# Linformer decode on one core: two heads per tile on 64 partitions each, K in 512-column matmuls, V multiplied by p·F

## Chip, cores, metric

One core of one Trainium2 chip. The metric is the device time of one execution in microseconds (us). The "span" of a profile runs from the first to the last instruction of one execution; the time is about 2 us longer than the span. "PE" is TensorE; its "granted clock" is the share of its full clock that it was given.

## The reference

```python
B, H, Sq, Skv, Dh, R = 2, 16, 1, 8192, 256, 8          # all bf16
kp = einsum("rn,bhnd->bhrd", e_proj, k)                # E K : 8 x 256 per head
vp = einsum("rn,bhnd->bhrd", f_proj, v)                # F V : 8 x 256 per head
scores = einsum("bhqd,bhrd->bhqr", q, kp) * Dh ** -0.5 # 8 scores per head
o = einsum("bhqr,bhrd->bhqd", softmax(scores), vp)
```

There are 32 heads. Each has 4.19 MB of K and 4.19 MB of V, 268.4 MB in all, read once. Everything else is small. Note that p·(F V) = (p·F) V: once the 8 probabilities of a head are known, F can be folded to one weight per row of V.

## The kernel before

Sixteen pairs of heads. Four buffers of 32 KB per partition hold one head's K or V each, as 128 partitions x 64 rows x 256. Per pair they hold K0, K1, V1, V0 (c = 0..3), and a buffer is loaded again when its matmuls are done.

```python
for a in range(NPAIR):                      # SyncE: the loads
    for c in range(NS):                     # NS = 4
        if a >= 1: nc.sync.wait_ge(s_rd[c], a)
        if ...: nc.sync.dma_start(out=big[:, c], in_=src).then_inc(s_dma[c], 16)      # 4 MB
        else:   # last pair: pieces, g1="32,32", g2="32,16,16", g3="16,12,10,8,6,4,3,2,1,1,1"
            ...
with nc.tensor.Fori(0, NPAIR) as it:        # TensorE
    ...                                     # q matmul
    for c in range(NS):
        ...                                 # waits
        for gi, gs in enumerate(groups[c]):
            for _ in range(gs):
                if c < 2:      # K: E.T k, 256 columns
                    mm = matmul(acc_k[:, c*Dh:(c+1)*Dh], lhsT=wT[:, j, 0:R2:2], rhs=big[:, c, j, :], ...)
                elif c == 2:   # V of head 1: F.T v  -- needs no probabilities
                    mm = matmul(acc_v1, lhsT=wT[:, j, 1:R2:2], rhs=big[:, c, j, :], ...)
                else:          # V of head 0: (p.F) v -- needs the softmax
                    mm = matmul(o_ps[0], lhsT=wp[:, j:j+1], rhs=big[:, c, j, :], ...)
            if c == 2 and gi == 0: ...      # broadcast p of head 0 to 128 partitions (pb)
            if c == 3 and gi == 0: ...      # o of head 1 = p (F v)
        mm.then_inc(s_rd[c], 1)
```

VectorE (DVE) makes the scores, ScalarE the exponential, and DVE then multiplies F by p and sums over the 8 ranks (wtmp, wp32, wp). This chain runs while TensorE (PE) works on c = 2.

Of the kernel before, what the change touches and what calls it, by code (L numbers as in the profile page):

```python
# [13 lines left out]
CFG = dict(g1="32,32", g2="32,16,16", g3="16,12,10,8,6,4,3,2,1,1,1")  # L14
# [3 lines left out]
def kernel(  # L18
# [8 lines left out]
):  # L27
    nc = tc.nc
# [4 lines left out]
    assert Sq == 1 and Skv % P == 0  # L33
    J = Skv // P
    BH = B * H
    G = 2
    assert BH % G == 0 and G * Dh <= 512
    NPAIR = BH // G
    assert 2 <= NPAIR <= P
    R2 = 2 * R  # L40
    NS = 4
    scale = float(Dh) ** -0.5
    TQ = 32

    CH = (P // 2) // R
    assert R * CH * 2 == P and Skv % CH == 0
    XW = Skv // CH
    PIECE = min(XW, 512)
    assert XW % PIECE == 0
    NPIECE = XW // PIECE  # L50
# [3 lines left out]

    big = sb.tile([P, NS, J, Dh], BF16, name="kv")
    wT = sb.tile([P, J, R2], BF16, name="wT")
    st = sb.tile([P, XW], BF16, name="ef_stage")
    sel_ef = sb.tile([P, CH, R2], BF16, name="sel_ef")
    q16 = sb.tile([NPAIR, G * Dh], BF16, name="q16")
    sel_q = sb.tile([NPAIR, NPAIR, R], BF16, name="sel_q")  # L60
    q_sb = sb.tile([R, G * Dh], BF16, name="q_sb")
    ident_b = sb.tile([R2, R2], BF16, name="ident_b")
    sc_in = sb.tile([TQ, TQ], FP32, name="sc_in")
    sc_out = sb.tile([TQ, TQ], FP32, name="sc_out")
    p_in = sb.tile([TQ, TQ], FP32, name="p_in")
    p_out = sb.tile([TQ, TQ], FP32, name="p_out")
    prod = sb.tile([R, G, Dh], FP32, name="prod")
    nmax = sb.tile([G, 1], FP32, name="nmax")
    ssum = sb.tile([G, 1], FP32, name="ssum")
    rsum = sb.tile([G, 1], FP32, name="rsum")  # L70
    p_pv = sb.tile([R, G], BF16, name="p_pv")
    vp_sb = sb.tile([R, Dh], BF16, name="vp_sb")
    ones1 = sb.tile([1, P], FP32, name="ones1")
    wtmp = sb.tile([P, J, R], FP32, name="wtmp")
    wp32 = sb.tile([P, J], FP32, name="wp32")
    wp = sb.tile([P, J], BF16, name="wp")
    o_all = sb.tile([1, BH * Dh], BF16, name="o_all")

    wps = pp.tile([P, J, R2], BF16, name="wps")
    NB = 6  # L80
    banks = [pp.tile([R2, 512], FP32, name=f"bank{i}") for i in range(NB)]
    pb_t = pp.tile([P, R], FP32, name="pb")
    acc_k = banks[0][0:R, 0:G * Dh]
    acc_v1 = banks[1][0:R, 0:Dh]
    o_ps = [banks[2][0:1, 0:Dh], banks[3][0:1, 0:Dh]]
    q_ps = banks[4][0:R, 0:G * Dh]
    pb = pb_t[:]

    ef_sb = big[:, NS - 1].rearrange("p j d -> p (j d)")[0:R2, 0:Skv]

    k_h = k.rearrange("b h (p j) d -> (b h) p j d", p=P)
    v_h = v.rearrange("b h (p j) d -> (b h) p j d", p=P)
    q_pr = q.rearrange("b h s d -> (b h s) d").rearrange("(a g) d -> a (g d)", g=G)
    o_v = out.rearrange("b h s d -> s (b h d)")
    e_st = e_proj.rearrange("r (c x) -> (r c) x", c=CH)
    f_st = f_proj.rearrange("r (c x) -> (r c) x", c=CH)

    def parse(key, fallback):
        tp = [int(x) for x in CFG[key].split(",")]
        return tp if sum(tp) == J else fallback  # L100

    def geometric():
        tp, rem = [], J
        while rem > 0:
            s_ = max(1, (rem * 3) // 10)
            tp.append(s_)
            rem -= s_
        return tp

    half = [J // 2, J - J // 2] if J >= 2 else [J]  # L110
    groups = [[J], parse("g1", half), parse("g2", half), parse("g3", geometric())]
    assert all(sum(g_) == J for g_ in groups)

    with tc.tile_critical(name="main"):
        sem = lambda n: nc.alloc_semaphore(f"lr_{n}")
        s_dma = [sem(f"dma{s}") for s in range(NS)]
        s_grp = [[sem(f"g{c}_{i}") for i in range(len(groups[c]))] for c in range(NS)]
        s_rd = [sem(f"rd{s}") for s in range(NS)]
        s_st, s_q, s_mm, s_qb, s_k0 = sem("st"), sem("q"), sem("mm"), sem("qb"), sem("k0")
        s_out = [sem(f"out{i}") for i in range(2)]  # L120
        s_pool, s_dve, s_act, s_tr = sem("pool"), sem("dve"), sem("act"), sem("tr")
        s_pv, s_pb = sem("pv"), sem("pb")

        cnt = {"dve": 0, "act": 0, "mm": 0}
        ND, NA = 11, 5

        def dve(inst):
            inst.then_inc(s_dve, 1)
            cnt["dve"] += 1
            return cnt["dve"]  # L130

        def act(inst):
            inst.then_inc(s_act, 1)
            cnt["act"] += 1
            return cnt["act"]

        npool = 0
        nc.gpsimd.memset(sel_ef[:], 0.0).then_inc(s_pool, 1); npool += 1
        nc.gpsimd.memset(sel_q[:], 0.0).then_inc(s_pool, 1); npool += 1
        nc.gpsimd.memset(ident_b[:], 0.0).then_inc(s_pool, 1); npool += 1  # L140
        nc.gpsimd.wait_ge(s_pool, npool)
        nc.gpsimd.affine_select(
            out=sel_ef[:], in_=sel_ef[:], compare_op=ALU.not_equal, fill=1.0,
            base=0, pattern=[[-1, CH], [-CH, R], [-(P // 2), 2]], channel_multiplier=1,
        ).then_inc(s_pool, 1); npool += 1
        NPOOL_EF = npool
        nc.gpsimd.affine_select(
            out=ident_b[:], in_=ident_b[:], compare_op=ALU.not_equal, fill=1.0,
            base=0, pattern=[[-1, R2]], channel_multiplier=1,
        ).then_inc(s_pool, 1); npool += 1  # L150
        NPOOL_ID = npool
        nc.gpsimd.affine_select(
            out=sel_q[:], in_=sel_q[:], compare_op=ALU.not_equal, fill=1.0,
            base=0, pattern=[[1, NPAIR], [0, R]], channel_multiplier=-1,
        ).then_inc(s_pool, 1); npool += 1
        nc.gpsimd.memset(sc_in[:], 0.0).then_inc(s_pool, 1); npool += 1
        nc.gpsimd.memset(p_in[:], 0.0).then_inc(s_pool, 1); npool += 1
        nc.gpsimd.memset(ones1[:], 1.0).then_inc(s_pool, 1); npool += 1
        NPOOL = npool

        while cnt["dve"] < ND:
            nc.vector.sem_inc(s_dve, 1)
            cnt["dve"] += 1

        bank_busy = [None] * 4
        nc.tensor.wait_ge(s_st, 32)
        nc.tensor.wait_ge(s_pool, NPOOL_EF)
        for c in range(CH):
            for h in range(NPIECE):
                i = cnt["mm"]  # L170
                b = i % 4
                if bank_busy[b] is not None:
                    eng, c_ = bank_busy[b]
                    nc.tensor.wait_ge(s_act if eng == "act" else s_dve, c_)
                nc.tensor.matmul(banks[b][0:R2, 0:PIECE], lhsT=sel_ef[:, c, :], rhs=st[:, h * PIECE:(h + 1) * PIECE],  # L175
                                 start=True, stop=True).then_inc(s_mm, 1)
                cnt["mm"] += 1
                dst = ef_sb[:, c * XW + h * PIECE:c * XW + (h + 1) * PIECE]
                if i % 2 == 0:
                    nc.scalar.wait_ge(s_mm, cnt["mm"])  # L180
                    bank_busy[b] = ("act", act(nc.scalar.copy(out=dst, in_=banks[b][0:R2, 0:PIECE])))
                else:
                    nc.vector.wait_ge(s_mm, cnt["mm"])
                    bank_busy[b] = ("dve", dve(nc.vector.tensor_copy(out=dst, in_=banks[b][0:R2, 0:PIECE])))  # L184

        nc.tensor.wait_ge(s_pool, NPOOL_ID)
        nc.tensor.wait_ge(s_act, cnt["act"])
        nc.tensor.wait_ge(s_dve, cnt["dve"])
        tr = None
        for j in range(J):  # L190
            tr = nc.tensor.transpose(out=wps[:, j, :], in_=ef_sb[:, j::J], identity=ident_b[:])  # L191
        tr.then_inc(s_tr, 1)
        nc.scalar.wait_ge(s_tr, 1)
        act(nc.scalar.copy(out=wT[:], in_=wps[:]))  # L194
        A0 = cnt["act"]
        D0 = cnt["dve"]
        assert A0 + 1 - NA >= 0 and D0 + 1 - ND >= 0

        def tile_src(a, c):
            return (k_h[a * G + c] if c < 2 else v_h[a * G + (3 - c)])  # L200

        def out_dma(a_lo, a_hi, i):
            nc.sync.wait_ge(s_act, A0 + (a_hi - 1) * NA + 5)
            nc.sync.dma_start(out=o_v[:, a_lo * G * Dh:a_hi * G * Dh],
                              in_=o_all[:, a_lo * G * Dh:a_hi * G * Dh]).then_inc(s_out[i], 16)

        J0 = min(J // 8, J - 1) if NPAIR > 1 else 0
        if J0 > 0:
            nc.sync.dma_start(out=big[:, 0, 0:J0, :], in_=k_h[0][:, 0:J0, :]).then_inc(s_k0, 16)
        nc.sync.dma_start(out=st[0:P // 2, :], in_=e_st).then_inc(s_st, 16)  # L210
        nc.sync.dma_start(out=st[P // 2:P, :], in_=f_st).then_inc(s_st, 16)
        A_OUT = NPAIR - 2
        n_out = 0
# [168 lines left out]
```

## Time and profile before

| | before |
|---|---|
| time | 634.64 us, median of 3 (634.34 to 635.01) |
| span of the profile | 632.7 us |
| DMA in the middle | 431 to 432 GB/s |
| PE busy / mean granted clock | 82% / 0.943 |
| 4 MB transfer, issue to landing | 31 us |

From the page of the kernel before: the span, the busy time of PE, the forty slices (granted clock, DMA busy share, GB/s), the three costliest groups (busy us, mean ns of one, then the idle time before them and what ended it) and the issues of the large transfers.

```profile
span 632.7 us, 9355 instructions
...
PE 516.4 (82%) x4240; PEld 372.5 (59%) x4240; DVE 69.2 (11%) x184; ACT 39.6 (6%) x106; POOL 2.1 (0%) x13
...
PEclk9798999889989999989989999899899889988999
DMA  8999999999999999999999999999999999999996
GB/s 345 430 430 431 431 431 431 429 431 431 431 431 436 433 431 433 433 433 435 433 433 435 433 431 433 431 431 431 431 431 431 431 431 431 431 431 431 424 423 263
...
L266 PE MATMUL bank_85<-kv,wT 128*8 128x256 bf16 x2048 | 244.9, 284 | 46.9 <-DMA kv<-in_k_dram 46.9
...
L269 PE MATMUL bank_86<-kv,wT 128*8 128x256 bf16 x1024 | 124.8, 283 | 32.8 <-DMA kv<-in_v_dram 32.8
L272 PE MATMUL bank_87<-kv,wp 128*1 128x256 bf16 x1024 | 123.3, 280 | 25.2 <-DMA kv<-in_v_dram 23.5
...
kv<-in_k_dram SPq DMA_DIRECT2D x30, 4096.0 KB, 31.4
```

DMA is busy everywhere (share 1.00 and 432 and 431 GB/s in the two stretches of the middle shown below). All three matmul groups wait for transfers; the only other wait that the waits view gives them is 1.8 us for ScalarE (L272). One 4 MB transfer per 9.7 us is the pace: 38.9 us a pair.

Instructions in order of time (start us, duration us, engine, line, operation, shapes, count, idle before and its releaser), last pair of the kernel before:

```profile
599.77 14.13 PE L266 MATMUL bank_85<-kv,wT 128*8 128x256 bf16 x128 [1.77 <-DMA kv<-in_k_dram]
613.94 0.68 DVE L300 SCALAR_TENSOR_TENSOR prod<-bank_85,q_sb 8x512 f32<-8x512 f32 x1 [26.18 <-PE bank_85 L266]
...
614.44 3.65 PE L269 MATMUL bank_86<-kv,wT 128*8 128x256 bf16 x32 [0.54 <-DMA kv<-in_v_dram]
...
621.89 1.91 PE L272 MATMUL bank_87<-kv,wp 128*1 128x256 bf16 x16
...
623.92 5.90 PE L272 MATMUL bank_87<-kv,wp 128*1 128x256 bf16 x48
...
629.86 0.36 ACT L351 CAST o_all<-bank_87 1x256 bf16<-1x256 f32 x1 [5.46 <-PE bank_87 L272]
```

The chain starts at 613.94, and PE is on V from 614.44. PE starts on the last buffer at 621.89 and follows its small pieces; it is done at 629.8, and only the output's copy and store follow. The landing of the first V piece at 614.44, plus 6 MB at the stream's pace (14.6 us), puts the last landing at about 629.0. This is an estimate; by the trace the stream moves 58 GB/s from 628 to 629 us and 2 GB/s from 629 to 630.

### The profile page before, as it was taken

What the parts mean: (1) busy time and instruction counts of PE and PEld (TensorE: products, weight loads), DVE (VectorE), ACT (ScalarE), POOL (GpSimd) and SP (SyncE); (2) the same over time, 40 slices, a digit from 0 to 9 for tenths busy, and PEclk for the clock granted to TensorE, in tenths of its full rate; (3) what the DMA queues carried; (4) which work ended last, traced back from release to release, by engine and by line L of the source; (5) the groups of instructions that cost most, each with busy time, mean ns of one, the idle gap of its engine ahead of it and who ended that gap; (6) DMA issues with size and microseconds to landing.
All of it is one profiled execution on the core that took longest, in us unless ns stands there. A gap on an engine that the chain in (4) does not pass through costs nothing.

```text
span 632.7 us, 9355 instructions
## 1 busy us (share of the span) xinstructions
PE 516.4 (82%) x4240; PEld 372.5 (59%) x4240; DVE 69.2 (11%) x184; ACT 39.6 (6%) x106; POOL 2.1 (0%) x13
## 2 busy tenths in 40 slices
PE   5998788787787887897886878969868788687898
PEld 2666556566565664665655656646656556465675
DVE  3020100202002020110201002010020100201011
ACT  3100010000100001000000000000000000000100
POOL 1000000000000000000000000000000000000000
PEclk9798999889989999989989999899899889988999
DMA  8999999999999999999999999999999999999996
GB/s 345 430 430 431 431 431 431 429 431 431 431 431 436 433 431 433 433 433 435 433 433 435 433 431 433 431 431 431 431 431 431 431 431 431 431 431 431 424 423 263
DMA packets 11434, 268.80 MB, mean 425 GB/s; under 512 B 1298, under 2 KB 1954, under 8 KB 2851
## 3 DMA queue, kind: packets, MB, share of 16 engines
q1 hardware_dynamic: 11428, 268.74, 99.1%
q8 instruction: 2, 0.03, 0.0%
q14 instruction: 4, 0.03, 0.0%
HBM read 268.71 MB, written 0.02 MB: 425 GB/s over the span
## 4 chain that ended last, share of the span: by engine, by line
DMA 72%; PE 26%; issue 1%; DVE 0%; ACT 0%; SPq 0%
DMA kv<-in_v_dram 71%; PE bank_86 L269 20%; PE bank_85 L266 3%; PE bank_87 L272 1%; PE wps L191 1%; PE pb L277 1%; DMA ef_stage<-in_f_proj_dram 1%; DVE kv L184 0%; PE bank_85 L175 0%; PE bank_88 L175 0%; PE bank_87 L175 0%; PE bank_86 L175 0%; ACT wT L194 0%; PE bank_89 L250 0%; SPq L210 0%
## 5 line engine op out<-in xcount | busy, mean ns | idle before, releaser
L266 PE MATMUL bank_85<-kv,wT 128*8 128x256 bf16 x2048 | 244.9, 284 | 46.9 <-DMA kv<-in_k_dram 46.9
L266 PEld LDWEIGHTS bank_85<-kv,wT 128*8 128x8 bf16 x2048 | 182.6, 90 | 109.4 <-DMA kv<-in_k_dram 29.1
L269 PE MATMUL bank_86<-kv,wT 128*8 128x256 bf16 x1024 | 124.8, 283 | 32.8 <-DMA kv<-in_v_dram 32.8
L272 PE MATMUL bank_87<-kv,wp 128*1 128x256 bf16 x1024 | 123.3, 280 | 25.2 <-DMA kv<-in_v_dram 23.5
L269 PEld LDWEIGHTS bank_86<-kv,wT 128*8 128x8 bf16 x1024 | 90.0, 90 | 63.1 <-ACT p_in L317 30.2
L272 PEld LDWEIGHTS bank_87<-kv,wp 128*1 128x1 bf16 x1024 | 85.4, 86 | 60.0 <-issue 25.5
L300 DVE SCALAR_TENSOR_TENSOR prod<-bank_85,q_sb 8x512 f32<-8x512 f32 x16 | 10.9, 678 | 476.6 <-PE bank_85 L266 476.6
L317 ACT ACTIVATE p_in<-sc_out,nmax 2x8 f32<-2x8 f32 x16 | 4.8, 299 | 309.4 <-DVE nmax L310 309.4
L333 DVE TENSOR_TENSOR wtmp<-wT,pb 128x512 f32<-128x512 bf16 x16 | 11.0, 687 | 54.5 <-PE pb L277 54.5
L345 ACT CAST vp_sb<-bank_86 8x256 bf16<-8x256 f32 x16 | 5.8, 362 | 125.7 <-PE bank_86 L269 125.7
L336 DVE TENSOR_REDUCE wp_81<-wtmp 128x64 f32<-128x512 f32 x16 | 11.0, 686 | 0.5
L351 ACT CAST o_all<-bank_87 1x256 bf16<-1x256 f32 x16 | 5.8, 362 | 82.1 <-PE bank_87 L272 82.1
L304 DVE TENSOR_REDUCE sc_in<-prod 8x2 f32<-8x512 f32 x16 | 10.8, 674 | 0.6
L348 ACT CAST o_all<-bank_88 1x256 bf16<-1x256 f32 x16 | 5.8, 362 | 57.2 <-PE bank_88 L281 57.2
L294 ACT CAST q_sb<-bank_89 8x512 bf16<-8x512 f32 x16 | 9.2, 575 | 2.6 <-PE bank_89 L250 1.0
L175 PE MATMUL bank_85<-ef_stage,sel_ef 128*16 128x512 bf16 x4 | 2.3, 584 | 6.2 <-DMA ef_stage<-in_f_proj_dram 6.2
L250 PE MATMUL bank_89<-q_65,sel_q 16*8 16x512 bf16 x16 | 6.2, 387 | 1.4 <-ACT wT L194 1.4
L277 PEld LDWEIGHTS pb<-p_in,ones_79 1*128 1x128 f32 x32 | 4.7, 182 | 3.5 <-issue 3.3
L191 PE MATMUL wps<-ident_b,kv 16*128 16x16 bf16 x64 | 5.8, 230 | 0.9 <-DVE kv L184 0.9
L191 PEld LDWEIGHTS wps<-ident_b,kv 16*128 16x128 bf16 x64 | 5.8, 206 | 1.2 <-issue 1.2
L277 PE MATMUL pb<-p_in,ones_79 1*128 1x8 f32 x32 | 6.1, 262 | 0.0
L281 PE MATMUL bank_88<-vp_sb,p_pv 8*1 8x256 bf16 x16 | 4.7, 291 | 0.0
(36 smaller groups left out, 49.2 us busy)
## 6 DMA issues: line engine op xcount, KB each, us to landing
kv<-in_k_dram SPq DMA_DIRECT2D x30, 4096.0 KB, 31.4
kv<-in_v_dram SPq DMA_DIRECT2D x30, 4096.0 KB, 31.0
kv<-in_k_dram SPq DMA_DIRECT2D x2, 2048.0 KB, 29.1
kv<-in_k_dram SPq DMA_DIRECT2D x1, 3584.0 KB, 12.4
kv<-in_v_dram SPq DMA_DIRECT2D x3, 1024.0 KB, 26.7
kv<-in_v_dram SPq DMA_DIRECT2D x1, 2048.0 KB, 24.6
kv<-in_v_dram SPq DMA_DIRECT2D x1, 768.0 KB, 25.6
kv<-in_v_dram SPq DMA_DIRECT2D x1, 640.0 KB, 26.7
```

Of the source, the lines that this page charges most:

```text
L191: tr = nc.tensor.transpose(out=wps[:, j, :], in_=ef_sb[:, j::J], identity=ident_b[:])
L250: nc.tensor.matmul(q_ps, lhsT=sel_q[:, bass.ds(it, 1), :].rearrange("k a m -> k (a m)"), rhs=q16[:], start=True, stop=True).then_inc(s_qb, 1)
L266: mm = nc.tensor.matmul(acc_k[:, c * Dh:(c + 1) * Dh], lhsT=wT[:, j, 0:R2:2], rhs=big[:, c, j, :], start=(j == 0), stop=(j == J - 1))
L269: mm = nc.tensor.matmul(acc_v1, lhsT=wT[:, j, 1:R2:2], rhs=big[:, c, j, :], start=(j == 0), stop=(j == J - 1))
L272: mm = nc.tensor.matmul(o_ps[0], lhsT=wp[:, j:j + 1], rhs=big[:, c, j, :], start=(j == 0), stop=(j == J - 1))
L277: nc.tensor.matmul(pb, lhsT=ones1[0:1, :], rhs=p_in[0:1, 0:R], start=True, stop=True).then_inc(s_pb, 1)
L294: assert act(nc.scalar.copy(out=q_sb[:], in_=q_ps)) == A + 1
L300: assert dve(nc.vector.scalar_tensor_tensor(out=prod[:].rearrange("r g d -> r (g d)"), in0=acc_k, scalar=scale, in1=q_sb[:], op0=ALU.mult, ...
L304: dve(nc.vector.reduce_sum(out=sc_in[0:R, 0:G], in_=prod[:], axis=AX.X))
L333: assert dve(nc.vector.tensor_tensor(out=wtmp[:], in0=fT, in1=pb.unsqueeze(1).to_broadcast([P, J, R]), op=ALU.mult)) == D + 9
L336: assert dve(nc.vector.reduce_sum(out=wp32[:], in_=wtmp[:], axis=AX.X)) == D + 10
L345: assert act(nc.scalar.copy(out=vp_sb[:], in_=acc_v1)) == A + 3
```

## The change

Its intent: fewer and larger instructions, loops on ScalarE and VectorE as on TensorE, one accumulator for all outputs. A tile now holds two heads, each on 64 partitions with 128 rows per partition. K and V each have one buffer of 64 KB per partition, loaded as two halves of 32 KB that are released separately. K takes two rows per matmul (512 columns). V of both heads is multiplied by p·F. Core of the diff (set-up of E and F, the chain's details and semaphores cut):

```diff
-CFG = dict(g1="32,32", g2="32,16,16", g3="16,12,10,8,6,4,3,2,1,1,1")
+STEADY = (64, 64)
+LAST_V = (64, 24, 16, 10, 6, 4, 2, 2)
...
-    big = sb.tile([P, NS, J, Dh], BF16, name="kv")          # J = 64
+    kt = sb.tile([P, J, Dh], BF16, name="kt")               # J = 128
+    vt = sb.tile([P, J, Dh], BF16, name="vt")
...
+        nc.sync.dma_start(out=st[:, 0:R // 2, :], in_=e_v).then_inc(s_st, 16)   # 256 B pieces, were 2 KB
...
+        for a in range(NP):
+            for i, js in enumerate(STEADY):
+                if a > 0: nc.sync.wait_ge(s_kr[i], a)
+                load(kt, k_t[a], lo, j0 + js - lo, s_kd[i])
...         # the same for vt with s_vr; last pair: pieces LAST_V
+        with nc.tensor.Fori(0, NP) as it:
+            ...
+            for j in range(0, J, 2):
+                if j in steady_at: nc.tensor.wait_ge(s_kd[steady_at[j]], tk)
+                mm = nc.tensor.matmul(acc_k[:], lhsT=wk[:, j:j + 2, :]..., rhs=kt[:, j:j + 2, :]..., ...)
+                if j + 2 in steady_end: mm.then_inc(s_kr[steady_end[j + 2]], 1)
+            nc.tensor.wait_ge(s_p, t1)
+            ...                                             # pb: broadcast p, then
+            nc.tensor.wait_ge(s_w, t1)                      # the whole chain
+            for j in range(J):
+                ...
+                mm = nc.tensor.matmul(o_ps[:], lhsT=wp[:, j, :], rhs=vt[:, j, :], start=False, ...)
+                if j + 1 in steady_end: mm.then_inc(s_vr[steady_end[j + 1]], 1)
...
+        with nc.scalar.Fori(0, NP) as it:                   # were written out
+        with nc.vector.Fori(0, NP) as it:
```

## The prediction

> **What bounds it now.** The DMA engines. By the forty slices, DMA is 9 tenths or more busy nearly everywhere and moves 431-433 GB/s[...]. 268.4 MB of K and V at 431.5 GB/s are 622 us of the 632.7 us span. The pace is one 4 MB transfer per 9.72 us, 38.9 us per pair of heads. PE (82% busy by the page) waits for K or V in every tile by the waits view (46.9, 32.8 and 23.5 us), so it isn't the bound. Transfers are issued some 31 us before they land (DMA issues), so the queue is three deep.
>
> **What the change does not touch.** Bytes, 4 MB transfers, 32 KB per partition, four buffers. [...]I expect the same 9.7 us per transfer.
>
> **What it changes.**
> 1. K: 64 matmuls of 512 columns for 128 of 256. The old pitch is 14.13 us/128 = 110 ns; I estimate 217 ns for 512 columns: 13.9 us a pair, as before.
> 2. V: both heads now need softmax(p) times F before their first matmul. Before, the tile of F matmuls (3.65 us per 32) ran during the softmax chain, hiding it. Now PE stands still from the last K matmul to the first V matmul. Chain, from DVE durations of before: 0.68 + 0.67 + 0.20 + three small ones 0.5, exp 0.30, three small ones 0.55, broadcast matmuls 0.6, product and sum over F twice as wide (0.69 each for 512 elements; estimate 1.22 each for 1024), two copies 0.5, gaps: about 7.3 us.
> 3. [...]In this trace 32 matmuls after 2.8 us idle took 5.32 us against 3.65: add about 1.9 us per pair.
> 4. PE per pair: 13.9 + 14.1 + 0.5 + 7.3 + 1.9 = 37.7 us against 38.9 of DMA. So the middle stays DMA bound, just barely, and should cost nothing.
> 5. Start: projections come as 256 B pieces, not 2 KB (1024 packets of them)[...]. The quicker set-up of weights (PE begins K at 14-15 us, not 21) gains nothing, since DMA bounds.
>
> **The tail is on the critical path.** Before, the last V piece is used 0.4 us after landing; landing pace puts that at about 629 us. In the new order the last K half lands two transfers earlier, near 609.6 (+1.5). Then K matmuls 7.0, chain 7.3, 128 V matmuls 16.0 end at 639.9 (+1.5), some 10 us after the last byte; output copy and store 2.9 as before. Span 642.8 + 1.5 = 644.3 against 632.7; the time is 1.9 above the span.
>
> **Prediction: 646.5 us (+1.9%), 8 in 10 between 641 and 654.** Chances: faster 0.03, within 2% 0.55, slower 0.42 (the limit is 647.3).
>
> **Right if:** windows in the middle show 431 GB/s and a 38.9 us period; in the last 35 us DMA goes quiet about 10 us before the last V matmul; the chain of waits ends in PE V matmuls preceded by DVE products and sums, not by a V transfer; the granted clock dips at each V start. **Wrong if:** the middle's GB/s falls (PE and chain period over 38.9: each excess us costs up to 16), or the 64 KB row stride in HBM slows reading; then over 650. If the chain is shorter, or PE stays at full clock, 641-644.
>
> What could mislead me: chain steps twice as wide are scaled, not measured; the 256 B pieces have no counterpart in this trace; the clock after idle varies between tiles (5.32 or 3.65 us).

The sum came to 609.6 + 7.0 + 7.3 + 16.0 = 639.9 us for the end of V, 642.8 us with copy and store, 644.3 us with the 1.5 us more at the start, and 646.2 us with the 1.9 us between span and time. The reason for the 1.5 us, the 256 B pieces, was a guess, tested in experiment 5. For the other 1.9 us, those of the slow start, the trace of before shows 5.32 - 3.65 = 1.67 us in the example given, and 15.98 - 14.13 = 1.85 us for the first 128 K matmuls, from 21.25 us (granted clock 0.50 from 20.7 to 24.1 us). That the rate of the stream could not rise was not shown; slices of experiment 6 moved 442 GB/s.

## The result

After: 645.95 us, median of 4 (644.67 to 646.32), beside 634.49 us (4 runs) for the kernel before on the same chip. The ratio is 1.0176, interval 1.0162 to 1.0191: slower, clear of the noise, though under 2%. The prediction, 646.5 (+1.9%), was right.

From the page of the kernel after, the parts shown before:

```profile
span 642.9 us, 7074 instructions
...
PE 498.4 (78%) x3185; PEld 317.6 (49%) x3185; DVE 97.3 (15%) x225; ACT 16.2 (3%) x36; POOL 8.5 (1%) x13
...
PEclk9979989797997979989798897979979798897989
DMA  8999999999999999999999999999999999999990
GB/s 337 434 427 434 432 430 432 432 434 426 436 432 432 428 434 428 436 428 434 428 438 428 434 428 434 432 430 432 428 436 428 434 428 438 428 432 430 436 399 6
...
L213 PE MATMUL o_ps<-vt,wp 128*32 128x256 bf16 x2048 | 258.7, 295 | 62.5 <-DVE wp L279 62.5
...
L197 PE MATMUL acc_k<-kt,wk 128*32 128x512 bf16 x1024 | 228.2, 381 | 14.2 <-DMA kt<-in_k_dram 14.2
...
L204 PE MATMUL pb<-prow,ones_80 1*64 1x8 f32 x64 | 5.0, 222 | 51.1 <-DVE prow L270 51.1
...
kt<-in_k_dram SPq DMA_DIRECT2D x31, 4096.0 KB, 31.5
```

The stream is the same up to the last two slices: there it moves 399 and 6 GB/s, where before it moved 423 and 263. The new wait is L213 <- DVE wp: PE stands 62.5 us for the chain, 3.9 us a pair, and another 51.1 us (3.2 us a pair) for the first part of the chain, before the broadcast (L204). What is left of waiting for K is 14.2 us, in 15 waits. So PE has only 14.2/15 = 0.95 us a pair to spare.

Stretches of the middle (length, busy time and count of PE, PEld, DVE, ACT, POOL, then granted clock, DMA share, GB/s), before and then after:

```profile
20.00:320.00 300.00, 247.28 (x2026) 179.19 (x2027) 31.95 (x88) 16.09 (x47) 0.00 (x0) 0.94 1.00 432
320.00:600.00 280.00, 227.64 (x1880) 164.57 (x1879) 27.97 (x77) 15.67 (x45) 0.00 (x0) 0.95 1.00 431
```

```profile
20.00:320.00 300.00, 235.07 (x1494) 148.39 (x1493) 48.02 (x112) 5.74 (x15) 0.00 (x0) 0.90 1.00 432
320.00:600.00 280.00, 224.99 (x1457) 145.47 (x1455) 42.03 (x98) 5.53 (x14) 0.00 (x0) 0.90 1.00 432
```

Nothing was lost or won there. The last pair of the kernel after, in order of time:

```profile
609.58 7.08 PE L197 MATMUL acc_k<-kt,wk 128*32 128x512 bf16 x32 [0.72 <-DMA kt<-in_k_dram]
616.77 0.68 DVE L249 SCALAR_TENSOR_TENSOR prod<-acc_k,q_sb 32x512 f32<-32x512 f32 x1 [31.94 <-PE acc_k L197]
...
619.85 0.28 PE L204 MATMUL pb<-prow,ones_80 1*64 1x8 f32 x4 [3.19 <-DVE prow L270]
620.18 1.22 DVE L273 TENSOR_TENSOR wtmp<-fw,pb 128x1024 f32<-128x1024 bf16 x1 [0.39 <-PE pb L204]
621.44 1.22 DVE L276 TENSOR_REDUCE wp_82<-wtmp 128x128 f32<-128x1024 f32 x1
...
623.25 0.44 DVE L279 CAST wp<-wp_82 64x128 f32 x1
...
624.04 15.70 PE L213 MATMUL o_ps<-vt,wp 128*32 128x256 bf16 x128 [3.90 <-DVE wp L279]
639.78 0.36 ACT L231 CAST o_sb<-o_ps 32x256 bf16<-32x256 f32 x1 [20.55 <-PE o_ps L213]
```

And the stream over that time (same columns as the stretches above):

```profile
624.00:626.00 2.00, 1.96 (x10) 1.39 (x11) 0.00 (x0) 0.00 (x0) 0.00 (x0) 0.50 1.03 397
626.00:628.00 2.00, 2.00 (x14) 1.52 (x13) 0.00 (x0) 0.00 (x0) 0.00 (x0) 0.68 0.42 148
628.00:630.00 2.00, 2.00 (x21) 1.77 (x19) 0.00 (x0) 0.00 (x0) 0.00 (x0) 1.00 0.03 9
```

The stream is practically empty from 628 us. PE goes on with V until 639.7. The sum of the tail, from the lines above:

| step, last pair of after | us | until |
|---|---|---|
| last K half lands (PE waited 0.72 for it) | | 609.58 |
| 32 K matmuls | 7.1 | 616.7 |
| chain, PE idle but for the broadcast (3.19 + 0.28 + 3.90) | 7.37 | 624.04 |
| 128 V matmuls, the first at half clock | 15.7 | 639.74 |
| PE's end in the kernel before | | 629.8 |

That is 9.9 us later at PE's end, and the spans differ by 10.2 us.

One more thing is in this trace. The 128 V matmuls of a pair take different times; here are three pairs in a row (PE alone):

```profile
235.46 15.44 PE L213 MATMUL o_ps<-vt,wp 128*32 128x256 bf16 x128 [3.89 <-DVE wp L279]
...
274.28 16.48 PE L213 MATMUL o_ps<-vt,wp 128*32 128x256 bf16 x128 [3.90 <-DVE wp L279]
...
313.14 15.84 PE L213 MATMUL o_ps<-vt,wp 128*32 128x256 bf16 x128 [3.90 <-DVE wp L279]
```

Without idling, 128 of them take 14.1 us (measured below), so a pair pays 1.3 to 2.8 us for starting at half clock (shortest V 15.44, longest 16.94; in the three stretches of the last V above, the granted clock is 0.50, 0.68 and 1.00); this is called the cold start below. The steps are regular: after the first they are 0.6 to 0.7 less from pair to pair, or about 1.0 more, with a pair every 38.86 us. What sets them no trace here shows. Nor is it shown how long PE must stand still for a cold start: in the kernel before, PE stood for only 1.88 us before the K matmuls at 133.57 us and then ran at a granted clock of 0.50 (135 to 137 us), 64 matmuls in 8.81 us and not 7.15; after 2.75 us before V at 153.00 it stayed at full clock (1.00, 32 in 3.65 us). The spread of the times does not show that the last V, which is on the critical path, draws a lot: the runs of the kernel after spread over 1.65 us, but those of the kernel before, too, over 0.8 to 2.2 us in later rounds of 7 to 9.

### The profile page after: what moved, and what is told of

The parts are those of the page before. It is cut to its first block, busy times and chain, and to the rows that moved or that the text cites. A ratio compares the mean times of both kernels' runs of the same rounds, so it can differ in the third digit from the quotient of the medians.

```text
span 642.9 us, 7074 instructions
## 1 busy us (share of the span) xinstructions
PE 498.4 (78%) x3185; PEld 317.6 (49%) x3185; DVE 97.3 (15%) x225; ACT 16.2 (3%) x36; POOL 8.5 (1%) x13
## 4 chain that ended last, share of the span: by engine, by line
DMA 73%; PE 24%; DVE 2%; issue 1%; SPq 0%; DVEq 0%; ACT 0%
DMA kt<-in_k_dram 73%; PE acc_k L197 19%; PE o_ps L213 5%; DVE wtmp L273 0%; DVE wp_82 L276 0%; DVE prod L249 0%; DVE sc_in L252 0%; DVE wp L279 0%; SPq L129 0%; PE pb L204 0%; DVE wp L264 0%; SPq L133 0%; SPq L142 0%; DVE sc_out L254 0%; SPq L132 0%
## 5 line engine op out<-in xcount | busy, mean ns | idle before, releaser
L213 PE MATMUL o_ps<-vt,wp 128*32 128x256 bf16 x2048 | 258.7, 295 | 62.5 <-DVE wp L279 62.5
L213 PEld LDWEIGHTS o_ps<-vt,wp 128*32 128x32 bf16 x2048 | 213.5, 105 | 104.7 <-issue 63.5
L197 PE MATMUL acc_k<-kt,wk 128*32 128x512 bf16 x1024 | 228.2, 381 | 14.2 <-DMA kt<-in_k_dram 14.2
L197 PEld LDWEIGHTS acc_k<-kt,wk 128*32 128x32 bf16 x1024 | 97.1, 97 | 140.9 <-DMA kt<-in_k_dram 22.4
L249 DVE SCALAR_TENSOR_TENSOR prod<-acc_k,q_sb 32x512 f32<-32x512 f32 x16 | 10.9, 679 | 504.3 <-PE acc_k L197 504.3
L204 PE MATMUL pb<-prow,ones_80 1*64 1x8 f32 x64 | 5.0, 222 | 51.1 <-DVE prow L270 51.1
L204 PEld LDWEIGHTS pb<-prow,ones_80 1*64 1x64 f32 x64 | 3.5, 148 | 59.0 <-DVE prow L270 59.0
L273 DVE TENSOR_TENSOR wtmp<-fw,pb 128x1024 f32<-128x1024 bf16 x16 | 19.5, 1221 | 6.6 <-PE pb L204 6.6
L276 DVE TENSOR_REDUCE wp_82<-wtmp 128x128 f32<-128x1024 f32 x16 | 19.5, 1220 | 0.6
L227 ACT CAST q_sb<-q_ps 32x512 bf16<-32x512 f32 x16 | 9.2, 574 | 327.3 <-PE q_ps L190 327.3
L252 DVE TENSOR_REDUCE sc_in<-prod 32x1 f32<-32x512 f32 x16 | 10.8, 674 | 0.6
L278 DVE CAST wp<-wp_82 64x128 f32 x16 | 7.0, 437 | 2.2
L279 DVE CAST wp<-wp_82 64x128 f32 x16 | 7.1, 442 | 0.2
```

The lines of the kernel that those rows point to most:

```text
L197: mm = nc.tensor.matmul(acc_k[:], lhsT=wk[:, j:j + 2, :].rearrange("p j m -> p (j m)"), rhs=kt[:, j:j + 2, :].rearrange("p j d -> p (j d)" ...
L204: mm = nc.tensor.matmul(pb[g * PH:(g + 1) * PH, :], lhsT=ones1[:], rhs=prow[:, g, :], start=True, stop=True)
L213: mm = nc.tensor.matmul(o_ps[:], lhsT=wp[:, j, :], rhs=vt[:, j, :], start=False, stop=(j == J - 1), skip_group_check=True)
L227: nc.scalar.copy(out=q_sb[:], in_=q_ps[:]).then_inc(s_qa, 1)
L249: then(0, nc.vector.scalar_tensor_tensor(out=prod[:], in0=acc_k[:], scalar=scale, in1=q_sb[:], op0=ALU.mult, op1=ALU.mult))
L252: then(1, nc.vector.reduce_sum(out=sc_in[0:2 * GR, 0:1], in_=prod[:], axis=AX.X))
```

## The experiments

Theory: all of the loss lies after the last K half has landed (exposed chain, cold start, V matmuls after the last byte). Rivals: the stream has become later or slower (256 B pieces, row stride of 64 KB, small last pieces); or the loops with register addresses made the chain longer.

### 1. V with constant weights (wrong result on purpose)

```diff
-            nc.tensor.wait_ge(s_p, t1)
-            ...  # pb
-            nc.tensor.wait_ge(s_w, t1)
             for j in range(J):
+                if j == J // 2: ...            # waits for s_p, and s_w of the pair before; pb
-                mm = nc.tensor.matmul(o_ps[:], lhsT=wp[:, j, :], rhs=vt[:, j, :], ...)
+                mm = nc.tensor.matmul(o_ps[:], lhsT=wk[:, j - j % 2:j - j % 2 + 2, :]..., rhs=vt[:, j, :], ...)
```

> V multiplied by constant weights of the same shape (wrong result on purpose), so V waits for its data only; the softmax chain still runs but PE does not stand for it. Tail theory (the 10 us are the exposed chain of 7.3 us, the half-clock start of 1.6 us, and V matmuls that then run after the last byte): V keeps up with its transfers and ends within 1 us of the last landing near 629 us; time back to 634.5, range 633.5 to 636. Rival, a later or slower stream (256 B pieces, 64 KB row stride): stays above 642, since nothing of the stream is changed.

Measured: 638.31 us (638.05 to 639.0), ratio 1.0059 (1.0042 to 1.0076). Taking away PE's wait for the chain, and with it the cold start, brings back about two thirds of the loss. The stream was not touched (432 and 431 GB/s in the two stretches), so a slower stream is not the cause of these two thirds. But the expectation was 634.5, and it was missed. Last pair:

```profile
618.88 7.15 PE L215 MATMUL o_ps<-vt,wk 128*32 128x256 bf16 x64 [1.03 <-DMA vt<-in_v_dram]
...
626.17 7.16 PE L215 MATMUL o_ps<-vt,wk 128*32 128x256 bf16 x64
...
633.37 0.36 ACT L233 CAST o_sb<-o_ps 32x256 bf16<-32x256 f32 x1 [12.96 <-PE o_ps L215]
```

The first V piece, 64 rows, lands at 618.88. From then PE has all 128 matmuls to do, 14.3 us, while only one transfer of 9.7 us is still to come. "V keeps up with its transfers" was the slip: a big first piece gives PE a backlog that it cannot work off before the last byte. The last 3.5 us between this run (633.3) and the kernel before (629.8) are this backlog.

### 2. PE kept busy during the chain

```diff
+            for _ in range(12): nc.tensor.matmul(ps_e[0:32, 0:4, :]..., lhsT=wk[:, 0:2, :]..., rhs=wk[:, 0:32, :]..., ...)
             nc.tensor.wait_ge(s_p, t1)
...
+            for _ in range(14): ...   # the same
             nc.tensor.wait_ge(s_w, t1)
```

> 26 matmuls of 512 columns on constants fill the two idle stretches of PE inside the softmax chain, so that V starts at full clock. Tail theory with the clock as a part of it: 128 V matmuls take 14.1 us instead of 15.7, the mean granted clock rises from 0.90 to above 0.97, and the time falls by 1.6 us to 644.3 (ratio to before about 1.0153), because only the last pair's V is on the critical path. If the half clock were not part of the loss: no change, 645.9. If it cost in each of the 16 pairs: 620, which the stream forbids.

Measured: 643.0 us (642.32 to 643.58), ratio 1.0129 (1.0112 to 1.0146), clock 0.984. The line that matters:

```profile
623.99 14.13 PE L221 MATMUL o_ps<-vt,wp 128*32 128x256 bf16 x128 [0.78 <-DVE wp L287]
```

V takes 14.13 us where it took 15.70. The gain is 3.0 us by the ratios (0.0047 x 634.6), more than the 1.6 expected. That expectation used the profiled run of after, which was its fastest (644.67); over the 16 pairs the cold start costs 1.3 to 2.8 us, 2.0 on the mean (258.7/16 - 14.13). The two intervals together leave about 1.4 us either way, so the gain agrees with this mean; between the two profiled executions it was 1.6 us (spans 642.9 and 641.3). The half clock is a real part of the loss, and useless matmuls buy it back.

### 3. The last V half in one piece

```diff
-LAST_V = (64, 24, 16, 10, 6, 4, 2, 2)
+LAST_V = (64, 64)
```

> The last V half in one piece of 64 instead of seven falling ones. Tail theory: PE reaches that half about 632 us, 3 us after its last byte, so the pieces buy nothing: no change, within 0.4 us of 645.9. Rival (the small last pieces drain slowly and set the end): a change of 1 us or more, either way.

Measured: 645.17 us (644.68 to 646.49), ratio 1.0169 (1.0152 to 1.0185). The difference of 0.0007 (0.4 us) is inside the intervals. The fine pieces at the end buy nothing in this kernel, because PE arrives after them.

### 4. A longer chain

```diff
             nc.vector.wait_ge(s_d[8], t1)
+            ...   # product and sum over F once more, with waits of their own
```

> Product and sum over F done twice in each pair: 2.5 us more of chain. In the middle PE waits 14.2 us for K over 15 pairs, 0.95 us a pair. If that is the whole headroom, PE and chain become the bound: period 38.9 + 1.55 = 40.4 us, time 645.9 + 2.5 + 15 x 1.55 = 671.7, range 667 to 675, and GB/s in the middle falls to about 415. If the middle had plenty of room (the stream bounds it comfortably): only the tail pays, 648.4.

Measured: 678.44 us (677.27 to 679.05), ratio 1.0682 (1.0665 to 1.07). The direction was right, and "plenty of room" is out: 2.5 us of chain cost 32 us. The size was above the range. At the period seen below, 40.96 us for the 16.78 MB of a pair, the stream is down to 410 GB/s (worked out). PE alone, one pair to the next:

```profile
305.59 13.99 PE L197 MATMUL acc_k<-kt,wk 128*32 128x512 bf16 x64
...
329.46 16.84 PE L213 MATMUL o_ps<-vt,wp 128*32 128x256 bf16 x128 [6.41 <-DVE wp L284]
...
346.55 13.99 PE L197 MATMUL acc_k<-kt,wk 128*32 128x512 bf16 x64
...
370.42 16.84 PE L213 MATMUL o_ps<-vt,wp 128*32 128x256 bf16 x128 [6.41 <-DVE wp L284]
```

From K to K is 346.55 - 305.59 = 40.96 us, and there is no wait for K any more. V takes 16.84 us in both pairs shown, near the slow end of its range, not the 16.2 that the headroom of 0.95 us was taken with: 38.86 + (2.5 - 0.95) + 0.6 = 41.0. From V to V the first periods are 41.05, 41.00, 40.98, 40.97 and then 40.96 to within 0.01, with V going from 16.93 to 16.84, so what is over 40.96 about halves each time. So this loop, bound by PE, settled at one period, here one with a slow V; why it settled there was not shown.

### 5. The 256 B pieces twice

```diff
         nc.sync.dma_start(out=st[:, R // 2:R, :], in_=f_v).then_inc(s_st, 16)
+        nc.sync.dma_start(out=st2[:, 0:R // 2, :], in_=e_v).then_inc(s_st2, 16)
+        nc.sync.dma_start(out=st2[:, R // 2:R, :], in_=f_v).then_inc(s_st2, 16)
```

> The 256 B pieces of e_proj and f_proj are loaded a second time, to a tile nobody reads, right behind the first: the cost of these 1024 pieces, measured by doubling. The last K half landed at 609.58 us where the pace of before put it at 609.55, so the small pieces seem to cost no more than their bytes: 262 KB at 431 GB/s, +0.6 us, range 0.4 to 1.2. The prediction's own estimate[...]: +2 us or more.

Measured: 645.11 us (644.96 to 646.89), ratio 1.0173 (1.0159 to 1.0187), against 1.0176. No cost is visible. With half-widths of 0.0014 a cost of 2 us (0.0032) would just have shown; 0.6 us could not. The profile decides no more: the last K half landed at 609.94 us, 0.4 us later than after's 609.58, but this landing varies between profiles whose early stream is the same, from 608.67 (experiment 3) to 610.41 us (experiment 10). The prediction's surcharge of 1.5 us was too high by these signs; that the pieces cost nothing is not shown.

### 6. Halves not released alone

```diff
-STEADY = (64, 64)
+STEADY = (128,)
```

> K and V tiles move and are released whole (8 MB, 64 KB per partition) instead of in halves. Reasoning: K is usable only when all of it has landed (T), matmuls end at T + 14.2, chain T + 21.6, V T + 37.3; the next V may be issued only then, 1.6 us before the queue runs dry at T + 38.9, [...]so a hole of about 1 us per pair; and the tail grows by one K half, 7.1 us. Time 646 + 7 + 13 = 666, range 655 to 672. If halves buy only the tail: 653. If halves buy nothing: 646.

Measured: 667.78 us (665.92 to 669.31), ratio 1.0521 (1.0499 to 1.0543), inside the range. A stretch of the middle (columns as above) shows a hole in the stream:

```profile
300.00:305.00 5.00, 5.00 (x48) 4.44 (x46) 0.00 (x0) 0.00 (x0) 0.00 (x0) 1.00 0.49 210
305.00:310.00 5.00, 5.00 (x27) 2.28 (x26) 0.00 (x0) 0.57 (x1) 0.00 (x0) 1.00 1.01 380
```

Such holes don't come in every pair. The spans differ by 21.9 us (664.8 and 642.9); 7.1 us of this are the 32 more K matmuls after the last landing of K, which leaves 14.8 us for a later landing, about 1 us a pair (estimate). The edit loads and releases whole tiles at once. Loading and release in halves is what makes two buffers enough; without it the change would have cost 5%, not 1.8%.

### 7. Finer pieces everywhere

```diff
-STEADY = (64, 64)
+STEADY = (64, 32, 16, 16)
```

> Each tile in pieces of 64, 32, 16, 16 instead of 64, 64. Tail theory: after the last K byte only 8 matmuls of 0.22 us remain instead of 32, so the whole tail moves 5.3 us earlier: 640.6, range 639.5 to 641.8, ratio to before about 1.0095. Rival, a slower stream: no gain, or a loss from smaller transfers (646 or more).

Measured: 646.13 us (645.3 to 647.43), ratio 1.0175 (1.0159 to 1.019). No gain; the expectation was missed. A stretch of the middle, and the last K:

```profile
320.00:600.00 280.00, 223.65 (x1447) 145.07 (x1446) 42.03 (x98) 5.53 (x14) 0.00 (x0) 0.90 1.01 429
```

```profile
603.75 13.99 PE L197 MATMUL acc_k<-kt,wk 128*32 128x512 bf16 x64 [1.27 <-DMA kt<-in_k_dram]
```

Two things ate the gain. The stream fell from 432 to 429 GB/s, so the first half of the last K landed at 603.75 us (in after it landed near 599.9, estimated as the second half's 609.58 less one transfer of 9.7). And the 64 K matmuls then ran without a stop: after a first piece of 64 PE has 14 us of work, more than the 9.7 us in which the rest lands, so it was never waiting for the small pieces. K ended at 617.7, 1 us later than after (616.7). It is the backlog of experiment 1 again. Whether the shorter rows or the number of transfers slowed the stream was not separated. The rival named "a loss from smaller transfers" predicted this time, but for a reason that lies in the edit and not in the change.

### 8. K at 256 columns

```diff
-    acc_k = pp.tile([2 * GR, 2 * Dh], FP32, name="acc_k")
+    acc_k = pp.tile([GR, Dh], FP32, name="acc_k")           # also q_ps, q_sb, prod, sel_q
...
-            for j in range(0, J, 2):
-                mm = matmul(acc_k[:], lhsT=wk[:, j:j + 2, :]..., rhs=kt[:, j:j + 2, :]..., ...)
+            for j in range(J):
+                mm = matmul(acc_k[:], lhsT=wk[:, j, :], rhs=kt[:, j, :], ...)
...                                                          # the addition of two halves of scores goes
```

> K as 128 matmuls of 256 columns onto 16 rows instead of 64 of 512 onto 32 rows; the scaled product and its sum run over 256 columns instead of 512, and the addition of the two halves goes. PE: 128 x 0.110 = 14.1 us against 64 x 0.2216 = 14.2, no difference. Chain: product and sum 0.27 us shorter each, one addition of 0.2 us gone: tail 0.7 us shorter, 645.2, range 644.7 to 645.6. If wide K matmuls save PE time that matters, this is slower than 646.

Measured: 644.86 us (643.7 to 645.02), ratio 1.0159 (1.0145 to 1.0172), against 1.0176. The median lies in the range given, but the intervals overlap, so the time alone does not prove a gain. The profile is clear: 64 K matmuls of 256 columns took 7.15 us, 32 of 512 take 7.08; and the chain, from the last K matmul to the first V matmul, took 6.64 us instead of 7.37. The wide K matmuls save PE nothing, and cost the chain 0.7 us: product and sum run over twice the columns, and the two halves must be added.

```profile
609.11 7.15 PE L193 MATMUL acc_k<-kt,wk 128*16 128x256 bf16 x64 [1.30 <-DMA kt<-in_k_dram]
...
622.90 15.83 PE L208 MATMUL o_ps<-vt,wp 128*32 128x256 bf16 x128 [3.90 <-DVE wp L271]
```

### 9. The last K ahead of a part of the V before it, first try

```diff
-STEADY = (64, 64)
-LAST_V = (64, 24, 16, 10, 6, 4, 2, 2)
+STEADY = (64, 32, 32)
+LAST_V = (64, 32, 12, 8, 5, 4, 2, 1)
+    wp2 = sb.tile([P, J, BH], BF16, name="wp2")             # V weights of the last pair
...     # loads: ..., K14, V14[0:96], K15, V14[96:128], V15
...     # PE:    ..., K14, V14[0:96], K15, V14[96:128] (the chain of pair 15 runs), V15
```

> The last pair's K is brought in front of the last quarter of the pair before's V (pieces 64, 32, 32; weights of the last pair in a tile of their own), so that PE has V matmuls to do while the last softmax chain runs, and the chain ends about when the first half of the last V lands. Tail theory: V keeps up with its transfers, ends within 1 us of the last landing: 634.5 or slightly less, range 633 to 636. Rival, a later or slower stream or slower loops: stays above 642.

Measured: 643.22 us (642.64 to 643.23), ratio 1.013 (1.0114 to 1.0145). A gain of 2.9 us where 11.4 were expected. The last V:

```profile
621.91 16.40 PE L222 MATMUL o_ps<-vt,wp 128*32 128x256 bf16 x128 [5.94 <-DMA vt<-in_v_dram]
```

The chain was hidden now: PE did not wait for it but for the transfer, 5.94 us. But again the first V piece was 64 rows, landing at 621.91, and 128 matmuls with a cold start (16.4 us) came after it. The pieces of 32 in all pairs also slowed the stream (431 and 429 GB/s in the two stretches).

### 10. ACT and DVE written out

```diff
-        with nc.scalar.Fori(0, NP) as it:
-            t1 = nc.scalar.snap(it + 1)
+        for it in range(NP):
+            t1 = it + 1
...     # the same on DVE
```

> The loops of DVE and ACT written out, PE's loop kept. Tail theory: chain the same but for register work in front of three of its instructions[...]: 645.5, range 645.0 to 646.0. Rival (the loops lengthen the chain by microseconds): below 644.

Measured: 645.89 us (644.6 to 646.34), ratio 1.0171 (1.0155 to 1.0187). No change. The loops on ACT and DVE cost nothing that can be seen in the time; in the profile the second part of the chain (PE's wait before V) is 3.79 us instead of 3.90. PE's loop was not tried.

### 11. The reordered end, with pieces that PE can keep up with

```diff
 STEADY = (64, 64)
-LAST_V = (64, 24, 16, 10, 6, 4, 2, 2)
+LAST_V = (32, 32, 32, 12, 8, 6, 4, 2)
...     # loads: ..., K14, V14[0:64], K15[0:64], V14[64:96], K15[64:96], K15[96:128], V14[96:128], V15 in pieces
...     # PE:    ..., K14, V14[0:64], K15, V14[64:96], pb, V14[96:128], V15
```

> The reordered end once more, after the first try failed because its last V still came in a first piece of 64 (landed 9.7 us before the end, with 14 us of matmuls and a cold start to do after it) and because pieces of 32 in all pairs slowed the stream from 432 to 429-431 GB/s. Now all pairs but the end keep pieces of 64; at the end the order is first half of the last K, third quarter of the V before, rest of the last K in two pieces, last quarter of that V, then the last V in pieces of 32, 32, 32, 12, 8, 6, 4, 2. Corrected tail rule (the end is the latest of: landing of a piece plus the PE work of everything after it): K ends 3.5 us after its last piece, the chain runs under V matmuls, PE reaches the last V about when its first piece lands and then keeps pace: V ends within 1 us of the last landing near 629 us, time 634.4, range 633.3 to 636. If it stays above 641, the tail is not where the 11 us are.

Measured: 635.99 us (635.46 to 636.17), ratio 1.0022 (1.0008 to 1.0036), at the upper edge of the range. Of the 11.2 us that after lost by its ratio (0.0176 x 634.6), 9.8 are back, with the same stream (432 and 431 GB/s), the same matmuls and the same loops but at the end. As in experiment 9, PE's last two pairs and DVE's last are written out; experiment 9 stayed at 643.22 us, so that alone is not the gain. The last V:

```profile
619.01 3.67 PE L271 MATMUL o_ps<-vt,wp 128*32 128x256 bf16 x32 [0.18 <-DMA vt<-in_v_dram]
...
623.92 7.16 PE L271 MATMUL o_ps<-vt,wp 128*32 128x256 bf16 x64 [1.25 <-DMA vt<-in_v_dram]
```

The last weights are ready before the second piece lands (PE waits for DMA at 619.01). The third piece of 32 lands at 623.92 and 64 matmuls follow.

### 12. The same with sixteens

```diff
-LAST_V = (32, 32, 32, 12, 8, 6, 4, 2)                     # against experiment 11
+LAST_V = (32, 32, 16, 16, 12, 8, 6, 4, 2)
```

> The reordered end with the last V in pieces of 32, 32, 16, 16, 12, 8, 6, 4, 2. In the run before, the third piece of 32 landed at 623.92 us and 64 matmuls of 7.15 us were still to do, ending at 631.07, some 2.5 us after the stream ran dry. By the corrected rule a piece of 16 lands about 2.4 us earlier, PE goes on with it, and V ends with the last landing, near 629: 1.9 us less, 634.1, range 633.5 to 635.0, level with the kernel before. If the reordered end has another floor: 636 again.

Measured: 635.17 us (634.88 to 635.96), ratio 1.0005 (0.9991 to 1.0019): level with the kernel before, but the median lies just above the range of 633.5 to 635.0, and the intervals of experiments 11 and 12 overlap. The last 96 V matmuls now run in one go:

```profile
619.34 10.65 PE L271 MATMUL o_ps<-vt,wp 128*32 128x256 bf16 x96 [0.18 <-DMA vt<-in_v_dram]
```

They end at 629.99, against 629.8 in the kernel before. The 1 us over the 629 expected is the rule once more: the second piece lands at 619.34, and all 96 matmuls after it take 10.65 us. No version here beats the kernel before by a margin that shows. Both ends stand on the same stream.

## Why the prediction was right

- **The bound.** The stream bounds the middle: right. 432 GB/s after, 431 to 432 before. The row stride of 64 KB in memory slows nothing.
- **K pitch.** 217 ns were estimated, 7.08/32 = 221 ns measured; no gain and no loss on PE, and experiment 8 confirms that the width does not matter (64 of 256 columns 7.15 us, 32 of 512 7.08).
- **Chain.** 7.3 us were estimated, 7.37 measured, partly by luck: the two strided copies took 0.44 us each instead of 0.25, the broadcast 0.3 instead of 0.6.
- **Cold start.** 1.9 us were estimated; 1.6 in the profiled tail, 1.3 to 2.8 over the pairs. Experiment 2 shows that it counts (V 14.13 us, not 15.70).
- **Barely bound.** PE with chain was put at 37.7 us a pair. It is 38.86 - 0.95 = 37.9. Experiment 4 shows how thin this is (2.5 us of chain cost 32 us).
- **Start.** The surcharge of 1.5 us for the 256 B pieces, a guess, was wrong: the last K half landed at 609.58, where 609.6 was said without the surcharge and 611.1 with it. That this agrees to 0.02 us is luck, since the landing varies by 1.7 us between profiles (experiment 5). Experiment 5 finds no cost. This is the term that was mis-sized. In the profiled execution it is the whole difference (span 642.9 us where 644.3 was said). The other three runs had spans of 643.7 to 644.2, so the median came nearer to the number than the terms were; longer cold starts (granted clocks of 0.898 and 0.899, not 0.904) or a later stream may have made up for it, and no trace of them shows which. PE's first K matmul came at 16.4 us and not at 14 to 15, without effect.
- **Tail.** V was to end 10 us after the last byte, at 639.9 us without that surcharge; it ended at 639.74. Experiments 1, 2, 11 and 12 show that this is where the loss is: hiding the chain and fitting the pieces brings it back.

What the prediction did not see is that the size of the first V piece is a second part of the tail. It counted "128 V matmuls" after the chain, and so had the sum right; but the reasoning "the chain is the cause" led to three expectations (1, 7, 9) that were too good. The rule that then held, in 11 and 12: PE's end is the latest, over all pieces, of its landing plus all PE work that comes after it.

## What to carry to other kernels

In a kernel bound by its stream, a change that leaves the stream alone, makes no hole in it (experiment 6) and makes no engine the bound (experiment 4), moved the time only at the end here: write down, for each of the last pieces, its landing plus the engine work that must follow it, and take the latest. Work that depends on a reduction over the tile just loaded needs other, already landed work beside it, or its whole latency is added at the end (7.37 us here); reordering the last loads gives it that work (with pieces that fit, experiment 11 got 9.8 us back). And an engine that looks 78% busy may have 2% to spare (0.95 of 38.86 us here) when its idle time is a dependency and not slack.
